# First layer of the first expert put between the count groups of the second routing round

## The chip, the cores and the metric

The kernel runs on one core of a Trainium2 chip. The core has a matrix engine (TensorE, here PE), a vector engine (VectorE, DVE), a scalar engine (ScalarE, ACT), GpSimd (POOL) and a queue engine (SyncE, SP), which work from queues of their own and wait for each other by semaphores. The metric is the device time of one execution, in microseconds (us); lower is better.

## The reference

The reference is attention with sink tokens, then a mixture of experts with greedy routing, then one with Sinkhorn weights. The attention has batch 2, 8 heads, 768 positions, head size 64, a window of 128 and 4 sinks. Its output is seen as 1536 tokens of 512 numbers. The part that the change touches is the greedy routing and its experts:

```python
cap = N // E                                   # 1536 // 8 = 192
flat = (x @ w_gate).flatten()
for idx in np.argsort(-flat):
    tok, e = idx // E, idx % E
    if assigned[tok] >= 0 or counts[e] >= cap: continue
    assigned[tok] = e; counts[e] += 1
for e in range(E):
    mask = assigned == e
    out[mask] = np.maximum(x[mask] @ w1[e], 0.0) @ w2[e]     # w1: 512x1024, w2: 1024x512
```

After it, eight experts are applied to all tokens and summed with weights from eight Sinkhorn steps.

## The kernel before

Attention comes first and fills about the first 150 us. It leaves the gate's logits `L` and, for the first routing round, a count that is made along the way (`first_count`). Then `routing_and_moe1` finds the greedy assignment in eight rounds, each of which closes one expert. In a round every token that is still free proposes to its best open expert. `count` finds for each token how many better proposals its expert has. `route` picks the expert that is filled, and the places of its tokens. `place_tokens` turns the places into a list of token numbers by one-hots (`ohs`) and a product, loads that expert's weights (`load_w`) and gathers its tokens (`gather`). `leave` takes the tokens and the expert out of the preferences `val`. `propose` takes the next maxima and spreads them over the partitions: the products L541 and the copies L542 give `row`.

`count` works on n chunks of 128 tokens, 12 in the first four rounds and 6 after `compact`. For each chunk DVE makes the comparison blocks `gt` (L559) and `g` (L560 and L562), which have four buffers each (`GB`), and PE multiplies them by the proposals into `cnt` (L568). Two chunks (`GC`) make one group of products. Within a group the products are given in reverse, so that they all stand behind the last block that DVE makes.

The expert's layers are in `moe1(r)`: L720 multiplies the gathered and turned tokens `xe` by the first weights in eight blocks of 128 (four matmuls each), ScalarE applies the Relu (L722) into `hT`, L731 multiplies by the second weights, and the gate logits of the next mixture follow (L742). `moe1(r - 1)` is written behind round r, so that its products fill PE during the routing. The weights of an expert come in four parts of 1 MB. Those of the first expert are split: part (0,0), the first half of the first layer, goes by SyncE's queue as soon as the expert is known, and the other three go by ScalarE's queue behind the last copy of `row`. `turn_tokens` (L704, L706) turns the gathered tokens; for the first expert it stands ahead of the second round's count.

The order of the instructions on each engine is set when the kernel is built: a planner takes what is ready by its own estimates, with the routing rounds under `tc.high_priority` ahead of the rest. `tc.issue_after(x)` puts instructions behind `x` on its engine, as an edge of order and not as a wait.

Of the kernel before, what the change touches and what calls it, by code (L numbers as in the profile page):

```python
# [8 lines left out]
F32 = mybir.dt.float32  # L9
# [3 lines left out]
AF = mybir.ActivationFunctionType  # L13
OP = mybir.AluOpType
# [6 lines left out]
def kernel(  # L21
# [16 lines left out]
    nc = tc.nc  # L38
    B, H, S, D = q.shape
    N, DM = out.shape  # L40
    E = moe_w_gate.shape[1]
    F = moe_w1.shape[2]
    P = 128
# [3 lines left out]
    CAP = N // E  # L47
# [15 lines left out]
    KD = DM // P  # L63
    KF = F // P
# [19 lines left out]
    slots = rp.tile([P, HC], BF, name="slots")  # L84
# [32 lines left out]
    val = rp.tile([P, NCH, E], F32, name="val")  # L117
# [300 lines left out]
    pm = ctx.enter_context(tc.tile_pool(name="pm", bufs=1, space=PSUM))  # L418
# [49 lines left out]
    def routing_and_moe1():  # L468
# [3 lines left out]
        mp = cx.enter_context(tc.tile_pool(name="mp", bufs=2))  # L472
# [12 lines left out]
        st = dict(n=NCH, L=L, val=val, code=code, prop=prop0, m=m0)  # L485
# [59 lines left out]
        def count(n, m, prop, row):  # L545

            cnt = ps.tile([P, n, E], F32, name="cnt", bufs=1)

            turned = st.pop("turned", None)
            with nullcontext() if turned is None else tc.issue_after(turned):  # L550
                nc.tensor.matmul(cnt.rearrange("p c e -> p (c e)"), zb, zb[:, :n * E], start=True, stop=False,
                                 skip_group_check=True)
            for c0 in range(0, n, GC):
                c1 = min(n, c0 + GC)
                blocks = []
                for c in range(c0, c1):
                    g = gp.tile([P, n, P], BF, name="g", bufs=GB)
                    gt = gp.tile([P, P], BF, name="gt", bufs=GB)
                    nc.vector.scalar_tensor_tensor(gt, row[:, c], m[:, c:c + 1], before, op0=OP.is_equal, op1=OP.mult)  # L559
                    nc.vector.tensor_scalar(g[:, :c + 1], row[:, :c + 1], m[:, c:c + 1], None, op0=OP.is_lt)  # L560
                    if c + 1 < n:
                        nc.vector.tensor_scalar(g[:, c + 1:], row[:, c + 1:], m[:, c:c + 1], None, op0=OP.is_le)  # L562
                    blocks += [(c, gt, prop[:, c, :])] + [(cc, g[:, cc, :], prop[:, c, :]) for cc in range(n)]

                first = None
                for cc, a, b in reversed(blocks):
                    with nullcontext() if first is None else tc.issue_after(first.ins):
                        mm = nc.tensor.matmul(cnt[:, cc, :], a, b, start=False, stop=(a is blocks[0][1] and c1 == n),  # L568
                                              skip_group_check=True)
                    first = first or mm  # L570
            return cnt
# [34 lines left out]
        def place_tokens(r, ft, t1, eh, code, n):  # L606

            def expert():
                return nc.vector.tensor_scalar(EIX[:, r:r + 1], t1[:, 1:2], -1.0, float(E), op0=OP.mult, op1=OP.add)

            if r == 0:
                expert()
                load_w(0, ((0, 0),))
            nc.vector.tensor_scalar(ft[:, 1], ft[:, 0], HC + 0.5, None, op0=OP.is_gt)
            nc.vector.scalar_tensor_tensor(ft[:, 2], ft[:, 1], -float(HC), ft[:, 0], op0=OP.mult, op1=OP.add)
            sm = ps.tile([P, 512], F32, name="sm", bufs=1)
            ohs = gp.tile([P, n, HC], BF, name="oh", bufs=OB)
            for c in range(n):
                nc.vector.tensor_scalar(ohs[:, c], slots, ft[:, 2, c:c + 1], None, op0=OP.is_equal)
            ch = gp.tile([P, n, 2, 2], BF, name="ch", bufs=OB)  # L620
            nc.vector.tensor_mul(ch[:, :, 1], code, ft[:, 1].unsqueeze(2).to_broadcast([P, n, 2]))
            nc.vector.tensor_sub(ch[:, :, 0], code, ch[:, :, 1])
            first = None
            for c in reversed(range(n)):
                with nullcontext() if first is None else tc.issue_after(first.ins):
                    mm = nc.tensor.matmul(sm[:HC, 0:4], ohs[:, c], ch[:, c].rearrange("p h a -> p (h a)"),
                                          start=(c == n - 1), stop=(c == 0), skip_group_check=True)
                first = first or mm
            st["placed"] = mm.ins
            at = rp.tile([HC, 2], F32, name="at", bufs=2)  # L630
            nc.vector.tensor_reduce(at, sm[:HC, 0:4].rearrange("p (h a) -> p h a", h=2), axis=AX.X, op=OP.add)
            known = nc.vector.tensor_copy(ixs[:, r, :], at)
            gather(r)
            if r:

                with tc.issue_after(known.ins):
                    expert()
                load_w(r, PARTS)

        def leave(ft, eh, n):  # L640

            val = st["val"]
            nc.vector.tensor_scalar(ft[:, 3], ft[:, 0], 0.5, None, op0=OP.is_gt)
            nc.vector.scalar_tensor_tensor(val, eh.unsqueeze(1).to_broadcast([P, n, E]), -100.0, val, op0=OP.mult,
                                           op1=OP.add)
            nc.vector.scalar_tensor_tensor(val, ft[:, 3].unsqueeze(2).to_broadcast([P, n, E]), -1000.0, val,
                                           op0=OP.mult, op1=OP.add)

        W, XG, YT = {}, {}, {}
        JH = KF // 2  # L650
        PARTS = ((0, 0), (0, 1), (1, 0), (1, 1))
        GC, GB = 2, 4
# [37 lines left out]
                nc.scalar.activation(xh, x, AF.Copy)  # L690
                nc.vector.tensor_sub(xl, x, xh.bitcast(F32))

        XE = {}

        def turn_tokens(r):

# [10 lines left out]
            if r == 0:  # L707
                st["turned"] = turned.ins

        def moe1(r):  # L710


            w1, w2 = W.pop(r)
            xe = XE.pop(r)
            hT = mp.tile([P, KF, CAP], F32, name="hT", bufs=1)
            for j0 in range(0, KF, 2):
                ph = pm.tile([P, 2, CAP], F32, name="mm", tag="mm", bufs=3)
                for j in (j0, j0 + 1):
                    for k in range(KD):
                        nc.tensor.matmul(ph[:, j - j0, :], w1[j // JH][:, k, j % JH * P:(j % JH + 1) * P], xe[:, k, :],  # L720
                                         start=(k == 0), stop=(k == KD - 1))
                nc.scalar.activation(hT[:, j0:j0 + 2, :], ph, AF.Relu)  # L722
            if r % 2 == 0:
                YT[r // 2] = mp.tile([P, KD, 2 * CAP], F32, name="yT", bufs=2)
            yT = YT[r // 2]
            s0 = r % 2 * CAP
            for k0 in range(0, KD, 2):
                py = pm.tile([P, 2, CAP], F32, name="mm", tag="mm", bufs=3)
                for k in (k0, k0 + 1):
                    for j in range(KF):  # L730
                        nc.tensor.matmul(py[:, k - k0, :], w2[j // JH][:, j % JH, k * P:(k + 1) * P], hT[:, j, :],  # L731
                                         start=(j == 0), stop=(j == KF - 1))
                nc.scalar.activation(yT[:, k0:k0 + 2, s0:s0 + CAP], py, AF.Copy)
                if k0 == 0 and r + 1 < E:
                    turn_tokens(r + 1)
            operands(r)

            c0, c1 = s0 // P, (s0 + CAP) // P
            pl = ps.tile([P, 2, E], F32, name="lg", bufs=1)
            for a in range(c0, c1):  # L740
                for k in range(KD):
                    nc.tensor.matmul(pl[:, a - c0, :], yT[:, k, a * P:(a + 1) * P], wg2[:, k, :],  # L742
                                     start=(k == 0), stop=(k == KD - 1))
            c = r // 2 * (2 * CAP // P)
            nc.vector.tensor_copy(L2[:, c + c0:c + c1, :], pl[:, :c1 - c0, :])

        for r in range(E):
            with tc.high_priority(offset=HP):
                got = route(r)
                place_tokens(r, *got)  # L750
                leave(got[0], got[2], got[4])
                if r + 1 == E // 2:
                    compact(NC2)
                if r + 1 < E:
                    propose()
                if r == 0:

                    with tc.issue_after(st["shown"]):
                        load_w(0, PARTS[1:], nc.scalar)
                    turn_tokens(0)  # L760
            if r == E - 1:
                rcx.close()
                pools.append(ctx.enter_context(tc.tile_pool(name="stg", bufs=1, side="right", reuse_waits="tile")))
            if r > 0:
                moe1(r - 1)
# [186 lines left out]
```

## Time and profile before

| what | value |
|---|---|
| median of 3 runs | 1417.15 us (1414.22 to 1417.31) |
| profiled execution, its own time | 1415.5 us |
| its span, first to last instruction | 1413.8 us |
| PE busy | 1375.5 us (97%) |
| DVE busy | 835.5 us (59%) |
| ACT busy | 459.8 us (33%) |
| POOL busy | 411.8 us (29%) |
| mean granted clock of PE | 0.984 |

The profile is of one execution; times in it count from its first instruction. A busy share is an average over attention, routing with the first experts (about 150 to 390 us) and the second mixture, which have different limits. Records of matmuls overlap, so their lengths don't add up to time. The granted clock is given as a share of 2.4 GHz.

### The profile page before, as it was taken

What the parts mean: (1) busy time and instruction counts of PE and PEld (TensorE: products, weight loads), DVE (VectorE), ACT (ScalarE), POOL (GpSimd) and SP (SyncE); (2) the same over time, 40 slices, a digit from 0 to 9 for tenths busy, and PEclk for the clock granted to TensorE, in tenths of its full rate; (3) what the DMA queues carried; (4) which work ended last, traced back from release to release, by engine and by line L of the source; (5) the groups of instructions that cost most, each with busy time, mean ns of one, the idle gap of its engine ahead of it and who ended that gap; (6) DMA issues with size and microseconds to landing.
All of it is one profiled execution on the core that took longest, in us unless ns stands there. A gap on an engine that the chain in (4) does not pass through costs nothing.

```text
span 1413.8 us, 20799 instructions
## 1 busy us (share of the span) xinstructions
PE 1375.5 (97%) x8243; PEld 1221.7 (86%) x8243; DVE 835.5 (59%) x1898; ACT 459.8 (33%) x975; POOL 411.8 (29%) x388
## 2 busy tenths in 40 slices
PE   7999599999989999999999999999999999999998
PEld 4667499999978989898889889898988988888987
DVE  4666788860376655555555555555555556555554
ACT  4666112222333332333233323323332332233321
POOL 1136200101332343232223322322343233223303
PEclk9999699999999999999999999999999999999999
DMA  6331343657210010001001100110010001000002
GB/s 141 90 79 39 129 148 131 232 180 227 90 31 31 30 45 31 30 31 45 30 31 32 44 31 30 35 41 30 31 44 32 31 30 45 31 30 31 15 1 89
DMA packets 87225, 87.37 MB, mean 62 GB/s; under 512 B 43864, under 2 KB 60248, under 8 KB 87128
## 3 DMA queue, kind: packets, MB, share of 16 engines
q1 hardware_dynamic: 82056, 73.45, 16.5%
q0 software_dynamic: 2944, 9.44, 2.0%
q10 hardware_dynamic: 2128, 3.16, 0.6%
q8 instruction: 64, 1.05, 0.3%
q14 instruction: 33, 0.27, 0.1%
HBM read 79.75 MB, written 6.30 MB: 61 GB/s over the span
## 4 chain that ended last, share of the span: by engine, by line
PE 93%; DVE 4%; ACT 1%; issue 1%; POOL 0%; DMA 0%; SPq 0%; POOLq 0%; DVEq 0%; ACTq 0%
PE pa L875 37%; PE X L818 19%; PE Z L818 9%; PE mm L720 6%; PE mm L731 6%; PE Y L818 5%; PE S L238 2%; PE o L293 2%; PE PT L280 1%; PE cnt L568 1%; PE ms L305 1%; PE tr L214 1%; PE lg L742 1%; POOL out_dram L888 0%; ACT pb L251 0%
## 5 line engine op out<-in xcount | busy, mean ns | idle before, releaser
L875 PE MATMUL pa<-w,h 128*128 128x512 f32 x2304 | 596.1, 394 | 0.0
L875 PEld LDWEIGHTS pa<-w,h 128*128 128x128 f32 x2304 | 426.9, 188 | 67.5 <-ACT h L825 0.3
L886 DVE SCALAR_TENSOR_TENSOR accs<-pa,Pm,accs 128x512 f32<-128x512 f32 x360 | 269.2, 748 | 212.2 <-PE pa L875 212.2
L826 DVE SCALAR_TENSOR_TENSOR h<-sum,h 128x384 fp32r<-128x384 f32 x192 | 155.4, 809 | 99.6 <-ACT h L825 99.3
L444 POOL TENSOR_TENSOR w1l<-r,w1h 128x512 fp32r<-128x512 f32 x64 | 64.2, 1023 | 450.6 <-ACT w1h L443 415.3
L825 ACT ACTIVATE h<-sum 128x384 fp32r<-128x384 f32 x192 | 100.5, 523 | 207.2 <-DVE sum L835 207.1
L461 POOL TENSOR_TENSOR w<-r,w 128x1024 fp32r<-128x1024 f32 x32 | 77.5, 2422 | 232.4 <-ACT w L460 232.4
L830 ACT ACTIVATE u<-X 128x384 f32<-128x384 f32 x64 | 31.5, 492 | 268.4 <-PE X L818 268.4
L720 PE MATMUL mm<-xe,wf 128*128 128x192 f32 x512 | 95.9, 337 | 0.0
L731 PE MATMUL mm<-hT,wf 128*128 128x192 f32 x512 | 91.5, 331 | 0.0
L444 POOL TENSOR_TENSOR w1l<-S,w1h 128x1024 fp32r<-128x1024 f32 x32 | 86.6, 2705 | 0.0
L720 PEld LDWEIGHTS mm<-xe,wf 128*128 128x128 f32 x512 | 83.1, 192 | 0.1
L731 PEld LDWEIGHTS mm<-hT,wf 128*128 128x128 f32 x512 | 82.6, 190 | 0.5
L835 DVE TENSOR_TENSOR sum<-Z,u 128x384 f32<-128x384 f32 x64 | 35.7, 557 | 58.4 <-ACT u L830 58.4
L668 POOL DMA_INDIRECT xg<-X,ixs x16 | 16.7, 1041 | 168.3 <-PE mm L704 60.6
L830 ACT ACTIVATE v<-X 128x384 f32<-128x384 f32 x64 | 31.4, 491 | 78.7 <-PE X L818 78.7
L251 ACT ACTIVATE pb<-pb,nb 128x264 f32<-128x264 f32 (+1 forms) x96 | 46.5, 489 | 14.2 <-DVE nb L246 14.2
L826 DVE SCALAR_TENSOR_TENSOR h<-X,h 128x384 fp32r<-128x384 f32 x64 | 35.7, 558 | 21.1 <-ACT h L825 21.1
L835 DVE TENSOR_TENSOR sum<-Z,v 128x384 f32<-128x384 f32 x64 | 35.7, 557 | 18.6 <-PE Z L818 18.5
L443 ACT ACTIVATE w1h<-r 128x512 fp32r<-128x512 f32 x64 | 30.2, 519 | 49.3 <-PE Z L818 46.2
L825 ACT ACTIVATE h<-X 128x384 fp32r<-128x384 f32 x64 | 31.5, 492 | 45.0 <-PE X L818 44.9
L241 DVE CUSTOM_DVE_ANT_0 pb<-S,M 128x264 f32<-128x264 f32 (+1 forms) x96 | 36.4, 403 | 13.5 <-PE S L238 12.8
(283 smaller groups left out, 2340.3 us busy)
## 6 DMA issues: line engine op xcount, KB each, us to landing
r<-in_moe_w_dram SPq DMA_DIRECT2D x64, 512.0 KB, 3.4
wf<-in_moe_w_dram SPq DMA_DIRECT2D x29, 1024.0 KB, 6.3
kn<-in_k_dram SPq DMA_DIRECT2D x12, 256.0 KB, 3.5
qn<-in_q_dram SPq DMA_DIRECT2D x12, 256.0 KB, 3.9
vn<-in_v_dram SPq DMA_DIRECT2D x12, 256.0 KB, 3.2
X<-xs POOLq DMA_DIRECT2D x12, 256.0 KB, 2.4
wf<-in_moe_w_dram ACTq DMA_DIRECT2D x3, 1024.0 KB, 10.3
xg<-X,ixs POOLq DMA_INDIRECT x16, 6.1
```

The costliest lines, as they stand in the source:

```text
L251: nc.scalar.activation(PB[c][:, h, :w], PB[c][:, h, :w], AF.Exp, bias=NB[c][:, 0, h:h + 1], scale=scale, accum_out=NB[c][:, 2, h:h + 1])
L444: nc.gpsimd.tensor_sub(w1[1][:, o:o + n], x, w1[0][:, o:o + n].bitcast(F32))
L461: nc.gpsimd.tensor_sub(w2[:, 1], r2, w2[:, 0].bitcast(F32))
L720: nc.tensor.matmul(ph[:, j - j0, :], w1[j // JH][:, k, j % JH * P:(j % JH + 1) * P], xe[:, k, :], start=(k == 0), stop=(k == KD - 1))
L731: nc.tensor.matmul(py[:, k - k0, :], w2[j // JH][:, j % JH, k * P:(k + 1) * P], hT[:, j, :], start=(j == 0), stop=(j == KF - 1))
L818: nc.tensor.matmul(acc_, w1[a][:, o, k, :], XO[x][t][b][:, k, :], start=(start and n == 0), stop=(stop and n == 3 * KH - 1), skip_group_ch ...
L825: nc.scalar.activation(t[:, 0], x, AF.Relu)
L826: nc.vector.scalar_tensor_tensor(t[:, 1], x, 0.0, t[:, 0].bitcast(F32), op0=OP.max, op1=OP.subtract)
L830: nc.scalar.activation(t, x, AF.Copy)
L835: nc.vector.tensor_add(t, a, b)
L875: nc.tensor.matmul(pa, HT[u, f, h][:, a, j * P:(j + 1) * P], w2[:, b, f, :], start=(n == 0), stop=(n == 3 * FP - 1))
L886: nc.vector.scalar_tensor_tensor(acc[:, c], pa, pe, acc[:, c], op0=OP.mult, op1=OP.add)
```

## The change

Of the first expert's first layer, the first four blocks (`EARLY`), sixteen matmuls, are given out at the end of round 0, right behind `turn_tokens(0)` and under the same high priority, and `moe1(0)` makes the rest. In the count of the second round the first product of each group is put behind one of them: the group of chunks 2 and 3 behind the fourth, that of 4 and 5 behind the eighth, that of 6 and 7 behind the twelfth, that of 8 and 9 behind the sixteenth. In all rounds the two operations for `ch` are written ahead of the one-hots, and the first two operations of `leave` are ordered behind the last one-hot; the third needs their results.

```diff
@@ count @@
             turned = st.pop("turned", None)
+            ahead = early if turned is not None else None
...
                 first = None
                 for cc, a, b in reversed(blocks):
-                    with nullcontext() if first is None else tc.issue_after(first.ins):
+
+                    after = first.ins if first else ahead[4 * c0 // GC - 1] if ahead and 0 < c0 <= 4 * GC else None
+                    with nullcontext() if after is None else tc.issue_after(after):
@@ place_tokens @@
-            for c in range(n):
-                nc.vector.tensor_scalar(ohs[:, c], slots, ft[:, 2, c:c + 1], None, op0=OP.is_equal)
             ch = gp.tile([P, n, 2, 2], BF, name="ch", bufs=OB)
             nc.vector.tensor_mul(ch[:, :, 1], code, ft[:, 1].unsqueeze(2).to_broadcast([P, n, 2]))
             nc.vector.tensor_sub(ch[:, :, 0], code, ch[:, :, 1])
+            for c in range(n):
+                shown = nc.vector.tensor_scalar(ohs[:, c], slots, ft[:, 2, c:c + 1], None, op0=OP.is_equal)
+            st["slots"] = shown.ins
@@ leave @@
-            nc.vector.tensor_scalar(ft[:, 3], ft[:, 0], 0.5, None, op0=OP.is_gt)
-            nc.vector.scalar_tensor_tensor(val, eh.unsqueeze(1).to_broadcast([P, n, E]), -100.0, val, op0=OP.mult,
-                                           op1=OP.add)
+            with tc.issue_after(st["slots"]):
+                nc.vector.tensor_scalar(ft[:, 3], ft[:, 0], 0.5, None, op0=OP.is_gt)
+                nc.vector.scalar_tensor_tensor(val, eh.unsqueeze(1).to_broadcast([P, n, E]), -100.0, val, op0=OP.mult,
+                                               op1=OP.add)
@@ moe1 @@
-        XE = {}
+        XE, HT = {}, {}
...
+        EARLY = 4
+
+        def first_layer(r, blocks):
+            w1, xe, hT = W[r][0], XE[r], HT[r]
+            made = []
+            for j0 in blocks:
                 ph = pm.tile([P, 2, CAP], F32, name="mm", tag="mm", bufs=3)
                 for j in (j0, j0 + 1):
                     for k in range(KD):
+                        made.append(nc.tensor.matmul(ph[:, j - j0, :], w1[j // JH][:, k, j % JH * P:(j % JH + 1) * P], xe[:, k, :],
+                                         start=(k == 0), stop=(k == KD - 1)).ins)
                 nc.scalar.activation(hT[:, j0:j0 + 2, :], ph, AF.Relu)
+            return made
...
+            if r not in HT:
+                HT[r] = mp.tile([P, KF, CAP], F32, name="hT", bufs=1)
+                first_layer(r, range(0, KF, 2))
+            else:
+                first_layer(r, range(EARLY, KF, 2))
+            w2 = W.pop(r)[1]
+            del XE[r]
+            hT = HT.pop(r)
@@ round 0 @@
                     turn_tokens(0)
+                    HT[0] = mp.tile([P, KF, CAP], F32, name="hT", bufs=1)
+                    early = first_layer(0, range(0, EARLY, 2))
```

## Rows read from the trace of the kernel before

**Rows 1.** The page, part 4: the chain that ended last, by engine.

```profile
PE 93%; DVE 4%; ACT 1%; issue 1%; POOL 0%; DMA 0%; SPq 0%; POOLq 0%; DVEq 0%; ACTq 0%
```

**Rows 2.** Busy time by stretches: length, engines (instructions), granted clock, DMA share, GB/s.

```profile
150.00:177.00 27.00, 12.39 (x163) 10.01 (x164) 21.72 (x81) 2.94 (x6) 6.54 (x10) 0.50 0.46 163
172.00:176.40 4.40, 0.89 (x27) 0.80 (x28) 4.40 (x11) 0.00 (x0) 0.00 (x0) 0.50 1.04 397
240.00:391.00 151.00, 150.92 (x1191) 147.43 (x1190) 72.94 (x280) 38.38 (x80) 26.29 (x23) 1.00 0.52 171
```

**Rows 3.** PE's waits in 150 to 184 us: total, times, longest.

```profile
PE sm L626 <- DVE ch L622: 4.6, 1, 4.6
PE cnt L568 <- DVE g L562: 3.9, 3, 1.8
...
PE bc L541 <- DVE m L534: 0.7, 1, 0.7
```

**Rows 4.** PE in order of time: start, us, line; in brackets the wait.

```profile
171.09 0.48 PE L568 MATMUL cnt<-prop,g 128*128 128x8 bf16 x12 [0.28 <-DVE g L562]
...
173.73 0.48 PE L568 MATMUL cnt<-prop,g 128*128 128x8 bf16 x12 [1.78 <-DVE g L562]
...
176.37 0.48 PE L568 MATMUL cnt<-prop,g 128*128 128x8 bf16 x12 [1.78 <-DVE g L562]
```

**Rows 5.** The chain that ended last, in order of time: start, us, what.

```profile
177.23 2.77 PE mm L720 x8
...
180.64 2.06 PE mm L720 x12
182.69 0.63 PE cnt L568 x26
```

**Rows 6.** Busy time by stretches, around the rise of the clock.

```profile
179.50:180.00 0.50, 0.50 (x9) 0.33 (x8) 0.50 (x2) 0.00 (x0) 0.00 (x0) 0.50 0.00 0
180.00:180.50 0.50, 0.50 (x26) 0.50 (x23) 0.50 (x4) 0.00 (x0) 0.00 (x0) 0.91 0.00 0
```

**Rows 7.** First weight part: issue by time, us to landing; ScalarE around `xe`.

```profile
160.46 0.40 SPq L661 DMA_DIRECT2D wf<-in_moe_w_dram  x1
...
wf<-in_moe_w_dram SPq DMA_DIRECT2D x1, 1024.0 KB, 4.9
...
169.96 0.87 ACT L706 ACTIVATE xe<-mm 128x384 f32<-128x384 f32 x2 [2.54 <-PE mm L704]
```

**Rows 8.** DVE in order of time: placing of round 0, count, end of count.

```profile
158.49 0.25 DVE L644 SCALAR_TENSOR_TENSOR val<-eh,val 128x96 f32<-128x96 f32 x1
...
158.94 0.17 DVE L614 TENSOR_SCALAR ft<-ft 128x12 f32<-128x12 f32 x1
159.02 0.17 DVE L643 TENSOR_SCALAR ft<-ft 128x12 f32<-128x12 f32 x1
...
159.74 0.25 DVE L646 SCALAR_TENSOR_TENSOR val<-ft,val 128x96 f32<-128x96 f32 x1
159.91 1.94 DVE L619 TENSOR_SCALAR oh<-slots,ft 128x96 bf16<-128x96 bf16 x12
161.76 0.16 DVE L622 TENSOR_TENSOR ch<-code,ch 128x24 bf16<-128x24 bf16 x1
...
163.07 0.16 DVE L631 TENSOR_REDUCE at<-sm 96x2 f32<-96x4 f32 x1 [0.69 <-PE sm L626]
...
173.59 0.35 DVE L559 SCALAR_TENSOR_TENSOR gt<-row,m,before 128x128 bf16<-128x128 f32 x1
...
178.61 0.35 DVE L562 TENSOR_SCALAR g<-row,m 128x256 bf16<-128x256 f32 x1
...
180.45 1.01 DVE L560 TENSOR_SCALAR g<-row,m 128x1536 bf16<-128x1536 f32 x1
183.36 0.26 DVE L583 SCALAR_TENSOR_TENSOR sel<-cnt,prop 128x96 f32<-128x96 f32 x1 [1.90 <-PE cnt L568]
```

**Rows 9.** Waits in 183 to 400 us, DVE's for the counts: total, times, longest.

```profile
DVE sel L583 <- PE cnt L568: 6.4, 5, 1.9
```

More of the change, by code (lines that the diff above doesn't have):

```diff
@@ L708, in turn_tokens @@
                 st["turned"] = turned.ins
[L710 to L716, printed above, removed]
+        EARLY = 4
[3 more added lines that the diff above has]
+            for j0 in blocks:
                 ph = pm.tile([P, 2, CAP], F32, name="mm", tag="mm", bufs=3)
@@ L719, in moe1 @@
                     for k in range(KD):
-                        nc.tensor.matmul(ph[:, j - j0, :], w1[j // JH][:, k, j % JH * P:(j % JH + 1) * P], xe[:, k, :],
-                                         start=(k == 0), stop=(k == KD - 1))
+                        made.append(nc.tensor.matmul(ph[:, j - j0, :], w1[j // JH][:, k, j % JH * P:(j % JH + 1) * P], xe[:, k, :],
+                                         start=(k == 0), stop=(k == KD - 1)).ins)
                 nc.scalar.activation(hT[:, j0:j0 + 2, :], ph, AF.Relu)
+            return made
+        def moe1(r):
+            if r not in HT:
[6 more added lines that the diff above has]
+            hT = HT.pop(r)
             if r % 2 == 0:
```

## The prediction

> **What bounds the kernel now.** I read the page first, then a table by stretches, the waits, and the order of time around the touched code. The chain that ended last lies to 93% on TensorE (PE) [rows 1], so the time is PE's work plus whatever PE waits for. The table [rows 2] says where it waits: from 240 to 391 us it is busy 150.92 of 151.00, but in 150 to 177 us only 12.39 of 27, at a granted clock of 0.50, the lower of its two levels (1.2 GHz). That stretch is the first round of routing and most of the second round's count, and it is the only part of the first MoE where work handed to PE can shorten the run.
>
> What PE waits for there is listed in [rows 3]: 4.6 us for the one-hots, 3.9 us in three pieces for `g`. In order of time [rows 4] the second round's count comes in groups of 26 matmuls (two chunks, 12+1 each); call them G0 to G5. G1 has a wait of 0.28 us, G2 and G3 each have one of 1.78, because VectorE (DVE) needs 2.64 us for two chunks of `g` (173.73 to 176.37). Only behind G3 does the first expert's layer (L720) begin, at 177.23 us in the chain by time [rows 5]. From there PE has no wait: eight L720, G4, twelve, G5, eight more.
>
> Two lengths must be kept apart. The records of L720 overlap, so what counts is how many fit into a stretch: 12 into 2.06 us at full clock, 0.172 each, and 8 into 2.77 us at the lower one, 0.346 each [rows 5]. A count group takes 0.63 us at full clock [rows 5] and 0.86 at the lower one (176.37 [rows 4] to 177.23). The clock rose near 180.05 us: 0.50 until 180.0, 0.91 in the half microsecond after it [rows 6], PE having run without a gap since 176.37.
>
> **The change, part by part.** *Sixteen L720 matmuls given out ahead.* They are the first four 128-wide blocks of the hidden layer, four matmuls each; none is added, so what counts is when they run. Of their operands, the weight part (0,0) is issued by SyncE at 160.46 us and lands 4.9 us later, at 165.4, and `xe` is copied by ScalarE from 169.96 us in 0.87 us, behind its own three weight issues [rows 7]. So they can run from about 170.4 (first half of `xe`) and 170.8 us. The other three parts, 3.15 MB at 397 GB/s [rows 2], take 7.9 us from 169.9, so until about 178 us nothing but these sixteen can be given to PE. No DMA is added or moved past another queue. The two Relu copies fall on a ScalarE that stands idle.
>
> The new edges hold G1 behind the fourth, G2 behind the eighth, G3 behind the twelfth, G4 behind the sixteenth. I take the order to be G0, four, G1, four, G2 and so on, and walk it at the lower clock with everything 0.15 us earlier (next part). G0 ends at 170.65. Four (4 x 0.346 = 1.38) and a group (0.86) take 2.24 us: G1 ends at 172.9, G2 at 175.1, G3 at 177.4, the last four at 178.75. DVE offers two chunks every 2.64 us, those for G2 at 173.6 and for G3 at 176.2, when PE is still at the four ahead of them (to 174.3 and 176.5), so PE doesn't idle. Queued behind each four is a group, and who waits for the group is DVE, by its four `g` buffers: chunk 6 can be written once G1 is done, 172.9, and DVE comes to it at 173.44 (173.59 before [rows 8]); so DVE isn't held, with 0.5 us to spare. G4's `g` is ready at 178.81 (178.61 + 0.35 - 0.15 [rows 8]), G4 ends at 179.65; G5's is ready at 181.31 (180.45 + 1.01 - 0.15), and G5 ends at 182.0. Before, G5 stood behind twelve L720 and ended at 183.32 (182.69 + 0.63 [rows 5]), and DVE idled 1.90 us for it [rows 8]. **First term: 1.32 us**, the 0.15 included.
>
> Second, the L720 done by then: 20 before; now 16 and those that fit between 179.65 and 181.31, 9 at full clock or 4 at the lower one. After nine us without a gap I take the full clock there, and 8 of them, hence 24. **Second term: 4 x 0.172 = 0.69 us.** Bounds: at the lower clock with 8 squeezed in, G5 slips to 183.3 and only the four are gained, 0.7 us in all; with twelve at full clock G5 slips by 0.4 and eight are gained, 2.3. Above all this stands what PE lost there at all: 3.84 us of waits, 4 x 0.23 for G0 to G3 and 8 x 0.174 for eight L720 at the lower clock, 6.1 us.
>
> The FP8 and Floating Point Precision page of the Trainium skill (TensorE Precision Notes) says that a true FP32 product takes four passes; 192 columns in four passes are, as an estimate from that page, 0.32 us at full clock and 0.64 at the lower one. By that four would take 2.56 us, and with a group 3.42, longer than DVE's 2.64: G5 would end near 186, some 2.7 us late, a rule against the change. The spacing of 0.172 in this trace doesn't bear it out.
>
> *`ch` ahead of the one-hots, `leave` behind them.* Ahead of the twelve one-hots DVE now runs L644, L643 and L646 (0.25, 0.17, 0.25 us), and behind them L622, for which PE's L626 waits [rows 8]. By the starts, L646 holds the one-hots up by 0.17 (159.74 to 159.91). L644 and L643 run where DVE would mostly have waited for the result before (L614 starts 0.45 behind L644, with a reduction between); I take 0.07 for both. L622 costs 0.07 behind the one-hots (it ends at 161.92, they at 161.85) and 0.18 ahead of them, since it needs L621's result. Net 0.17 + 0.07 + 0.07 - 0.18 = 0.13; I take **0.15 us**, once, in the first round. Bounds: 0, and the three whole, 0.67. Behind the one-hots the three cost some 0.45 us ahead of the next proposal, but there DVE idled 0.69 us until PE's L626 was done [rows 8], which hides them; with that cover gone, `m` and the row broadcast L541 would come 0.3 us later (0.45 - 0.15). In later rounds PE is full and the 0.15 is worth nothing.
>
> VectorE: DVE Perf Modes of the Trainium skill (The DRAIN you can't avoid) holds that the next operation doesn't start until the pipe is empty; then each of the three would free its whole length, this part would be worth 0.67 and the sum 2.5. That L643 starts 0.08 behind L614 in this trace [rows 8] speaks against it.
>
> **Sum:** 1.32 + 0.69 = 2.0 us. After G5 PE is the bound until 391 us, and DVE has room: in the later rounds it waits 6.4 us in five pieces for the counts alone [rows 9]. So the lead is kept. The profiled execution took 1415.5 us (span 1413.8), which becomes 1413.5; the median of the runs shown is 1.65 us higher, so against it I forecast 1417.15 - 2.0 = **1415.1 us**.
>
> **The rivals.** *A: the sixteen run as one block behind G0.* No edge holds them behind a group, and all are ready together. Then they end at 170.65 + 16 x 0.346 = 176.2, G1 at 177.0; DVE stops ahead of chunk 6 from 173.44 to 177.0, and G5 ends near 185.6, 2.3 us later than before. But PE has no gap: from 177.9 (G2) to 185.6, less 3 x 0.63, it does 33 more L720, 49 in all, against 30 before at that time. That is 19 x 0.172 = 3.3, less 0.45 for the two steps of routing (`sm`) that it is behind, 2.8 us won, as long as DVE's room [rows 9] takes up the 2.3. Time 1414.3. For it: readiness; against it: nothing in the trace of before.
>
> *B: the moved `leave` shows on PE.* If no L720 stands between L626 and L541 in the new order, PE meets an `m` that is 0.3 us later, up to 0.67 if the three count whole, in each of seven proposals: 2.1 to 4.7 us lost against 2.0 won, 1417.3 to 1419.9, slower; it decides from 0.29 us a round on. For it: PE waited 0.7 us for `m` in the first round [rows 3]. Against it: later no PE wait is in the table [rows 2].
>
> *C: the gain is only a swap.* The order behind G4 loses the L720 that went ahead, PE idles until G5, and 16 stand against 20: 1.32 - 0.69 = 0.6 us, time 1416.5. For it: PE's queue holds only what the order gives it, as the 1.78 us waits show [rows 4].
>
> *D: PE's lead is larger*, with the full clock from G1 on and L720 in every gap: up to 6.1 us, 1411.1.
>
> **How the numbers follow.** Main case 0.45, A 0.18, B 0.12, C 0.17, D 0.08. The likeliest gives 1415.1, its own range 1414.3 to 1416.5. The runs shown spread over 3.1 us, so 0.3% (4.25 us) is about what can be told from no change. 1411.6 to 1418.6 leaves out the end of D, the upper part of B and some scatter. Faster by over 0.3% needs D, or A with scatter: 0.14. Slower by over 0.3% needs more than B's upper end, an order I don't foresee: 0.07. Within 0.3%: 0.79.
>
> **What would show it.** Right: L720 from about 170.6 us on, the 1.78 us waits for `g` gone, G5 ending near 182, DVE's 1.90 us wait at L583 cut to about 0.7, the span near 1411.8, PE still full to 391. A full clock before 178 would speak for D; a DVE gap near 173.5 with a block of sixteen for A; a wait of L541 for `m` in later rounds for B; a PE wait ahead of G5 for C. The forecast is wrong if the new order moves other work of the first MoE too, which the trace of before can't show.

## Result and the profile after

The changed kernel takes 1429.55 us (median of 4 runs, 1429.15 to 1434.15) against 1417.23 us before; the ratio is 1.0103, interval 1.0089 to 1.0117. It is slower by 1%, 12.3 us by the medians and 14.6 by the ratio, which is not that of the medians, where 2 us were to be won; that is outside the range. The profiled execution is the longest of the four, 1434.15 us with a span of 1432.4.

To see where the time went I cut each trace at two starts that every version has: the copy of the first count (L361, on DVE) and the first product of the Sinkhorn part (`gmx` on PE). Columns are us; "route 1 to 3" are the starts of the product `sm<-red` of the second to fourth round, counted from that copy.

| kernel | up to the copy | copy to Sinkhorn | behind it | route 1 | route 2 | route 3 |
|---|---|---|---|---|---|---|
| before | 154.7 | 247.2 | 1011.9 | 29.9 | 57.5 | 84.2 |
| after | 156.5 | 262.1 | 1013.8 | 32.1 | 68.3 | 105.1 |

Of 18.6 us, 14.9 lie in the first MoE; the attention, which the change doesn't touch, took 1.8 more in this execution, and the part behind 1.9. The second routing is 2.2 us late, the third 10.7, the fourth 20.9. PE's waits from 150 to 400 us say what stands there now (line, what it waited for: total, times, longest):

```profile
PE mm L709 <- DMA xg<-X,ixs: 9.1, 5, 4.4
...
PE bc L541 <- DVE m L534: 1.3, 1, 1.3
```

The 3.9 us of waits for `g` [rows 3] are gone, as forecast. In their place stand 9.1 us for `xg`, the gathered tokens, 8.3 of them behind the first round, where no wait was before. Here is PE in order of time:

```profile
172.73 2.93 PE L724 MATMUL mm<-xe,wf 128*128 128x192 f32 x8 [0.26 <-ACT xe L711]
175.46 0.51 PE L571 MATMUL cnt<-prop,g 128*128 128x8 bf16 x12
...
176.20 2.72 PE L724 MATMUL mm<-xe,wf 128*128 128x192 f32 x8
178.75 0.44 PE L571 MATMUL cnt<-prop,g 128*128 128x8 bf16 x12
...
197.10 1.14 PE L748 MATMUL mm<-hT,wf 128*128 128x192 f32 x6
202.67 0.42 PE L709 MATMUL mm<-ident,xg 96*128 96x96 f32 x1 [4.43 <-DMA xg<-X,ixs]
203.42 1.38 PE L709 MATMUL mm<-ident,xg 96*128 96x96 f32 x7 [0.33 <-DMA xg<-X,ixs]
204.59 2.18 PE L748 MATMUL mm<-hT,wf 128*128 128x192 f32 x6
206.57 0.51 PE L571 MATMUL cnt<-prop,g 128*128 128x8 bf16 x12
```

Two things are to be seen. The products ahead stand where I put them, eight records, a group, eight records, a group. And at 198.2 us PE comes to the turning of the second expert's tokens (L709) and stands for 4.8 us. Behind it in the queue wait 32 records of the second layer (L748) and the third round's first count group, whose last block DVE has made by 200.6 us. The chunks' buffers are not freed, so DVE stops too. By stretches (granted clock is the third number from the end):

```profile
198.20:202.70 4.50, 0.07 (x2) 0.03 (x1) 3.77 (x7) 0.49 (x1) 0.00 (x0) 0.98 1.05 358
202.70:207.00 4.30, 3.97 (x29) 3.56 (x30) 0.00 (x0) 1.39 (x3) 0.00 (x0) 0.50 1.05 403
```

After that stand PE works at the lower clock, 0.50. DVE, busy 3.77 of the 4.5 us, is then held up for the whole of 202.7 to 207. The next round repeats it (2.6 and 1.0 us). From 185 to 300 us the mean granted clock is 0.93 where before it was 1.00: some 16 us at half speed, an estimate from these two means of up to 8 us lost beside the 8.3 us of waits; the lead that PE had won pays a part of it back.

Why the gather is late is in GpSimd's rows and in the DMA share of the stretch, 1.05:

```profile
195.12 0.92 POOL L673 DMA_INDIRECT xg<-X,ixs  x1 [26.89 <-DVE pl L533]
196.34 0.92 POOL L673 DMA_INDIRECT xg<-X,ixs  x1 [0.30 <-PE bc L541]
...
xg<-X,ixs POOLq DMA_INDIRECT x2, 7.3
```

It takes 7.3 us to land (median of the two), while 4 MB of the same expert's weights are on the DMA engines; in the first round of before, where hardly any weights ran beside it (their first part landed at 165.4, a microsecond behind the issue of the gather), it took 3.1. In the second round of before, beside the same 4 MB, it was slow too, 6.3 us, but PE came late enough:

```profile
192.51 0.92 POOL L668 DMA_INDIRECT xg<-X,ixs  x1 [0.30 <-issue]
...
195.45 0.44 PE L568 MATMUL cnt<-prop,g 128*128 128x8 bf16 x12
...
197.49 0.45 PE L568 MATMUL cnt<-prop,g 128*128 128x8 bf16 x12
...
199.85 0.66 PE L704 MATMUL mm<-ident,xg 96*128 96x96 f32 x6
```

Before, PE came to this place 45.1 us behind the copy of the first count, with the second gather issued at 37.8; now at 41.7, with the gather issued at 39.8. PE is 3.4 us earlier, the gather 2.0 later, and the margin, about a microsecond before, has become a wait of 4.8. Of the 3.4 some 1.3 come from the order: two count groups of the third round stood ahead of the turning before (195.45 and 197.49) and stand behind it now.

### The profile page after: what moved, and what is told of

The parts are those of the page before. It is cut to its first block, busy times and chain, and to the rows that moved or that the text cites. A ratio compares the mean times of both kernels' runs of the same rounds, so it can differ in the third digit from the quotient of the medians.

```text
span 1432.4 us, 20802 instructions
## 1 busy us (share of the span) xinstructions
PE 1390.5 (97%) x8243; PEld 1232.7 (86%) x8243; DVE 838.4 (59%) x1898; ACT 460.8 (32%) x975; POOL 410.5 (29%) x388
## 3 DMA queue, kind: packets, MB, share of 16 engines
q8 instruction: 64, 1.05, 0.3%
## 4 chain that ended last, share of the span: by engine, by line
PE 92%; DVE 4%; DMA 2%; issue 1%; ACT 1%; POOL 1%; SPq 0%; ACTq 0%; POOLq 0%; DVEq 0%
PE pa L894 37%; PE X L837 18%; PE Z L837 9%; PE mm L724 6%; PE mm L748 6%; PE Y L837 5%; PE S L238 2%; PE o L293 2%; PE PT L280 2%; DMA xg<-X,ixs 1%; PE cnt L571 1%; PE ms L305 1%; PE tr L214 1%; PE lg L759 1%; POOL out_dram L907 0%
## 5 line engine op out<-in xcount | busy, mean ns | idle before, releaser
L748 PE MATMUL mm<-hT,wf 128*128 128x192 f32 x512 | 98.3, 342 | 0.0
L748 PEld LDWEIGHTS mm<-hT,wf 128*128 128x128 f32 x512 | 86.2, 198 | 0.3
L854 DVE TENSOR_TENSOR sum<-Z,v 128x384 f32<-128x384 f32 x64 | 35.7, 557 | 18.6 <-PE Z L837 18.5
```

What stands on the lines that cost most here:

```text
L854: nc.vector.tensor_add(t, a, b)
```

## The experiments

**The two parts alone.** First the order of `ch` and `leave`, without the products ahead:

```diff
+            for c in range(n):
+                shown = nc.vector.tensor_scalar(ohs[:, c], ...)   # behind ch
+            st["slots"] = shown.ins
...
+            with tc.issue_after(st["slots"]):                     # leave, first two operations
```

> The kernel before with the order of place_tokens and leave changed alone. Theory 1 (TensorE comes too soon to the turning of the next expert's tokens and its queue stands until their gather lands; this needs the products given ahead): within 0.3% of before, 1414 to 1420 us, no wait of TensorE for a gather of over 1 us behind the first round. Theory 2 (leave behind the one-hots delays m and the rows in every round): most of the loss is here, 1423 us or more.

Measured: 1421.94 us, ratio 1.0045 (1.0028 to 1.0061). Neither theory: TensorE has no long wait for a gather, as theory 1 says (0.6 us once, in the first round), but the part is no neutral one. DVE's rows (of the whole change, this part is the same there) show why:

```profile
164.72 0.16 DVE L635 TENSOR_REDUCE at<-sm 96x2 f32<-96x4 f32 x1 [0.68 <-PE sm L630]
164.80 0.24 DVE L531 TENSOR_REDUCE mx<-val 128x12 f32<-128x96 f32 x1
...
165.66 0.25 DVE L534 TENSOR_REDUCE m<-pl 128x12 f32<-128x96 f32 x1
```

In the kernel before they stood so:

```profile
161.85 0.24 DVE L531 TENSOR_REDUCE mx<-val 128x12 f32<-128x96 f32 x1
162.12 0.26 DVE L532 SCALAR_TENSOR_TENSOR prop<-val,mx 128x96 bf16<-128x96 f32 x1
...
163.43 0.25 DVE L534 TENSOR_REDUCE m<-pl 128x12 f32<-128x96 f32 x1
```

There `mx` and `prop` ran ahead of `at` and so during its wait of 0.69 us [rows 8]. With `leave` behind the one-hots the planner puts `at` first; it waits for PE, and `mx` to `m` stand behind it. The wait that was to hide the three operations now stands ahead of what they delay. Counted from the copy of the first count, `m` starts at 9.15 us instead of 8.71, 0.44 later, where I forecast 0.15 earlier. Route 1 is at 32.0 (before 29.9), Sinkhorn at 250.8 (247.2).

`ch` alone, ahead of the one-hots, with `leave` as it was:

> The kernel before with ch ahead of the one-hots alone, leave as before. If the loss of the run with both was in leave, moved behind the one-hots and so behind the reduction that waits for TensorE: within 0.3% of before, 1413 to 1418 us, m at the same time behind the first count to 0.2 us. If it was in ch: 1419 us or more.

Measured: 1417.84 us against 1416.06, ratio 1.0019 (1.0008 to 1.0030), inside the expectation; PE's order is that of before, from the copy to the end, and Sinkhorn is at 248.1. So most of this part's loss comes with `leave`.

Then the products ahead with their edges, `ch` and `leave` in the old order:

> The kernel before with the sixteen products ahead and their edges alone, leave and ch in the old order. Theory 1: as slow as the whole change, 1426 to 1434 us, with the waits of 4 to 5 us and 2 to 4 us for the gather in the second and third round. Theory 2: within 0.3% of before.

Measured: 1428.34 us, ratio 1.0087 (1.0067 to 1.0107), as theory 1 says. PE's waits of this kernel:

```profile
PE mm L707 <- DMA xg<-X,ixs: 10.6, 6, 3.5
```

**The turning later in PE's queue.**

```diff
-                if k0 == 0 and r + 1 < E:
+                if k0 == KD - 2 and r + 1 < E:
                     turn_tokens(r + 1)
```

> The whole change, but the turning of the next expert's tokens is written behind the second half of the second layer instead of the first, so that sixteen more products and some count groups stand ahead of it. Theory 1: the waits for the gather go, and with them 8 us and the lower clock behind them: 1414 to 1421 us. Theory 3 (the count groups held behind the sixteen make the routing late, and that is the loss): stays at 1425 us or more, since the groups are held as before.

Measured: 1418.09 us, ratio 1.0014 (1.0004 to 1.0024): 1.03% has become 0.14%. The same stretch of this kernel, by busy time, which in the changed kernel has PE at 17.21 of 22 us and a clock of 0.84:

```profile
190.00:212.00 22.00, 21.97 (x260) 20.92 (x259) 19.76 (x57) 5.06 (x10) 1.84 (x2) 1.00 0.57 210
```

PE has no wait there any more; the copy to Sinkhorn takes 247.3 us, as before. Theory 3 falls: route 1 is as late as in the whole change (32.0), and the time is back all the same. The control, the late turning alone in the kernel before:

> The kernel before with the late turning alone, the control for the late turning. TensorE had no wait at the turning before, so nothing is to be won: 1414 to 1418 us. If the late turning is a gain of its own, 1412 us or less, and then it is no proof for theory 1.

Measured: 1416.2 us against 1416.06, ratio 1.0011 (0.9996 to 1.0025). It gains nothing by itself. And with the products ahead, but `leave` in the old order:

> The products ahead and their edges, leave and ch in the old order, the turning of the next tokens behind the second half of the second layer. Theory 1 (the loss is TensorE's queue standing at the turning) with leave as a smaller loss of its own: 2 to 4 us below the whole change with the late turning, 1412 to 1416 us, no wait for the gather over 1 us behind the first round. If the count groups held behind the products cost what the late routing suggests (2 us): 1416 to 1419 us.

Measured: 1416.02 us, ratio 0.9994 (0.9985 to 1.0003): 2.1 us below the median of the run with the new order of `leave`, and the same as before.

**The gather faster.** The turning stays where it is; SyncE's queue reads a few bytes of the gathered tiles ahead of the weights, and so waits for them:

```diff
+                for x in XG[r]:
+                    nc.sync.dma_start(seen[r:r + 1, :], x[0:1, 0:4])
                 load_w(r, PARTS)
```

> The whole change, and in each round but the first SyncE's queue reads a few bytes of the two gathered tiles ahead of the next expert's weights, so that these 4 MB start when the gather has landed. TensorE's order hardly changes. Theory 1 with the weights as what makes the gather slow: it lands about 3 us after its issue instead of 7, the two waits fall to about 1 us each and the clock stays up: 1417 to 1423 us. If the gather is as slow without the weights beside it: 1428 us or more.

Measured: 1427.48 us, ratio 1.0073 (1.0050 to 1.0097). This is no answer, because the edit didn't do what it was meant to. SyncE's queue in this kernel:

```profile
197.92 0.38 SPq L669 DMA_DIRECT2D wf<-in_moe_w_dram  x1
204.78 0.31 SPq L644 DMA_DIRECT2D seen<-xg  x1
205.28 0.40 SPq L669 DMA_DIRECT2D wf<-in_moe_w_dram  x1
```

One part of 1 MB had gone ahead of the reads, and beside it the gather took 6.6 us. With the weights ordered behind the second read:

```diff
+                for x in XG[r]:
+                    landed = nc.sync.dma_start(seen[r:r + 1, :], x[0:1, 0:4])
+                with tc.issue_after(landed.ins):
+                    load_w(r, PARTS)
```

> As the run that held SyncE's queue until the gather had landed, but now all four parts of the weights are ordered behind that; in the run before one part of 1 MB had slipped ahead. If the weights are what makes the gather slow, it lands some 3 us after its issue, the waits at the turning fall to 1 to 2 us and the time to 1420 to 1425 us. If the gather takes 5 us by itself, 1426 us or more.

Measured: 1415.9 us against 1416.06, ratio 1.0003 (0.9993 to 1.0014): the whole loss is gone, more than I expected. PE's order is that of the changed kernel, from the copy to the end; its rows, and SyncE's and the gather's:

```profile
196.88 1.14 PE L752 MATMUL mm<-hT,wf 128*128 128x192 f32 x6
199.17 0.30 PE L713 MATMUL mm<-ident,xg 96*128 96x96 f32 x1 [1.15 <-DMA xg<-X,ixs]
199.63 0.80 PE L713 MATMUL mm<-ident,xg 96*128 96x96 f32 x7 [0.16 <-DMA xg<-X,ixs]
...
199.14 1.35 SPq L644 DMA_DIRECT2D seen<-xg  x2
201.54 2.28 SPq L670 DMA_DIRECT2D wf<-in_moe_w_dram  x4
...
xg<-X,ixs POOLq DMA_INDIRECT x2, 3.8
```

The gather lands in 3.8 us instead of 7.3, the stand of 4.8 us is one of 1.3, and the clock stays at 1.00 in this stretch. The routing stays late (the fourth round 6.5 us, table below), so its lateness alone isn't the loss. The Trainium skill (DMA: Bandwidth & Descriptors, Issuing engines are not separate DMA queues) says that transfers started by different engines run on the same 16 DMA engines and interleave. The traces agree: GpSimd's gather takes 7.3 us beside SyncE's weights and 3.8 with these held back.

**What is left to win.** Three combinations and one control, each against a before of 1416.95 us. First the products ahead with their edges and the weights held, `ch` and `leave` in the old order:

> The products ahead with their edges, leave and ch in the old order, all weights of the later rounds ordered behind the gather. Theory 1 (the weights slow the gather that TensorE's queue stands at): the 10.6 us of waits fall to some 3 us, 1412 to 1417 us, so 10 us or more below the same kernel without the hold. Otherwise 1424 us or more.

Measured: 1415.25 us, ratio 0.9990 (0.9980 to 1.0001); waits for the gather 2.7 us instead of 10.6, as expected. The same with the late turning:

> As the run before it in this call, and the turning late as well: no wait for the gather behind the first round at all. If the lead that TensorE wins by the products is kept, 1412 to 1415 us, the fastest so far; if the routing, held up by the same products, eats it, the same as before, 1415 to 1418 us.

Measured: 1416.41 us, ratio 0.9987 (0.9975 to 0.9998). By its ratio the fastest of all, 0.13%, at the edge of what can be told; the median is only 0.5 us below the kernel before's, and inside the range that was given for no gain. The control, the weights held in the kernel before:

> The kernel before with the weights behind the gather alone, the control. TensorE had no wait for the gather behind the first round, so nothing changes: 1413 to 1418 us.

Measured: 1418.37 us, ratio 1.0004 (0.9994 to 1.0013): no gain without the products ahead, 0.4 us above the range expected. And the kernel with products ahead and weights held, without the edges:

```diff
-                    after = first.ins if first else ahead[4 * c0 // GC - 1] if ahead and 0 < c0 <= 4 * GC else None
+                    after = first.ins if first else None
```

> The products ahead without the edges, so that the planner sets them as one block of sixteen behind the fourth count group; old leave, weights behind the gather. If the edges make the second round's count late (by 1 to 2 us), the second routing comes earlier than with them by that much in spite of the block, and the time is 1412 to 1416 us; if the block holds the last groups up as much, no difference to the kernel with the edges.

Measured: 1417.91 us, ratio 1.0002 (0.9993 to 1.0011). The expectation missed: route 1 comes at 32.8, later than the 31.1 with the edges, and Sinkhorn at 248.9 against 246.2. In these traces the block of sixteen behind the fourth group is worse than the spread; by the times, whose intervals touch, that isn't settled.

The cuts of the other kernels, as in the first table:

| kernel | copy to Sinkhorn | behind it | route 1 | route 2 | route 3 |
|---|---|---|---|---|---|
| `ch` and `leave` alone | 250.8 | 1014.5 | 32.0 | 60.4 | 89.3 |
| `ch` alone | 248.1 | 1012.1 | 30.7 | 58.3 | 85.1 |
| products ahead alone | 258.9 | 1012.0 | 31.0 | 66.8 | 101.3 |
| whole change, late turning | 247.3 | 1014.5 | 32.0 | 59.9 | 88.5 |
| whole change, weights held | 247.6 | 1012.1 | 31.9 | 61.9 | 90.7 |
| products, late turning | 246.2 | 1012.2 | 30.4 | 57.7 | 87.2 |
| products, weights held | 246.2 | 1012.2 | 31.1 | 60.2 | 88.3 |
| late turning alone | 247.3 | 1011.3 | 30.6 | 58.3 | 86.3 |
| weights held alone | 248.0 | 1012.6 | 30.7 | 58.3 | 85.0 |

The kernels with `ch` alone and with the weights held alone have PE's order of before throughout, and yet their route 1 is 0.8 us and their Sinkhorn 0.8 to 0.9 us later than in the profiled execution of before. In that one the clock rose 25.4 us behind the copy, in these two at 27.2 and 27.3. So differences of this size between two rows are not the edit's.

## Why the prediction was wrong, step by step

*Where PE waits, and that filling the gaps takes the waits away:* right. The waits for `g` went, and the order was the one I walked, but that the last of the four fours ran between the products of G3.

*The price of the four products: wrong by a factor of two.* "0.172 each" is the price of a record, and a matmul of this type leaves two. The page after shows it as well as the one before:

```profile
L724 PE MATMUL mm<-xe,wf 128*128 128x192 f32 x512 | 96.9, 342 | 0.3 <-ACT xe L711 0.3
```

Eight experts of eight blocks of four matmuls are 256, and 512 records are there. So four cost 2.73 us at the lower clock (172.73 to 175.46), not 1.38, and with a group 3.5 (to 176.20), longer than DVE's 2.64 for two chunks. DVE, which was to have 0.5 us to spare, is held by its buffers, and G5's wait, which was to shrink to 0.7, is nearly as long as before:

```profile
179.26 0.35 DVE L560 SCALAR_TENSOR_TENSOR gt<-row,m,before 128x128 bf16<-128x128 f32 x1 [0.49 <-PE cnt L571]
...
182.94 0.35 DVE L560 SCALAR_TENSOR_TENSOR gt<-row,m,before 128x128 bf16<-128x128 f32 x1 [0.95 <-PE cnt L571]
...
187.34 0.26 DVE L586 SCALAR_TENSOR_TENSOR sel<-cnt,prop 128x96 f32<-128x96 f32 x1 [1.79 <-PE cnt L571]
```

G5 comes 2.2 us later instead of 1.3 earlier. By the parts alone, route 1 is at 31.0 with the products and at 32.0 with `ch` and `leave`, against 30.7 in the two kernels with PE's order of before, so the larger share of the delay is that of `leave`, and the doubled price cost little here: with the products alone the clock rose 20.2 us behind the copy, 7 us sooner than in those two. The rule of the Trainium skill that I set aside (FP8 and Floating Point Precision, TensorE Precision Notes, four passes) came within 8% of the trace: two records of 0.172 make 0.344 us a matmul at full clock, and 2.73/4 = 0.68 at the lower one, against the 0.32 and 0.64 estimated from that page.

*The second term, the L720 done by G5's end: mis-sized.* 48 records stand ahead of G5, 20 before. That is the 24 matmuls of the forecast, but the "20 before" were records, ten matmuls. So PE had won 28 x 0.172 = 4.8 us of work by G5's end, not 0.7; as G5 came 2.2 us later, that is a lead of some 2.6.

*The `leave` part: wrong in sign.* The placing did come earlier as forecast: `at` starts 8.21 us behind the copy instead of 8.35, 0.14 where 0.15 was taken. The cover named for the rest, DVE's 0.69 us, was real too, but the operation that waits moved ahead of those it was to cover. Rival B named the sign and the place, and put it in every round on PE; it showed as a later `m` and a later second round, 3.6 us up to Sinkhorn, or 2.7 to 2.8 against the two kernels with PE's order of before.

*"So the lead is kept" is the step that failed.* I asked whether DVE had room and not what PE would meet next in its queue. PE came to an operation that waits for a transfer 3.4 us sooner, the transfer was issued 2.0 us later, and the queue stood there with work behind it: 8.3 us of waits and the lower clock behind them, 14.9 us lost up to Sinkhorn. That the order of other work could move, as the turning and two count groups did, the prediction's last sentence had left open. That the order in the queue makes the loss is shown twice, by the late turning with its control and by the faster gather; that the weights make the gather slow is shown by the pair of holds. No rival named it: A held PE to be full as long as DVE had room, and D, the lead, counted it as pure gain. How the loss divides between the waits and the clock was not measured apart.

*Size.* With the trap taken away the products ahead bring about 0.1%, at the edge of what can be told: of the three kernels with `leave` in the old order and the edges, only one has an interval without 1 in it (0.9975 to 0.9998). By the cuts it is 1.1 to 1.8 us against the controls (246.2 against 247.3 with the late turning alone and 248.0 with the weights held alone), little more than two executions with one order differ by. That this is about what I forecast for the main case is luck, since both terms and the `leave` part were off. Where the rest of the lead goes is in part open. With the late turning the clock falls to 0.50 from 236.8 to 240.2 us and from 298.2 to 301.6, though PE stands nowhere there, an estimate of up to 3.4 us lost; with the weights held the gather still costs PE 1.3 us more than in the control.

## What to carry to other kernels

Work that fills an engine's idle time also brings that engine sooner to the next thing in its queue. Look for the first instruction there that waits for a transfer, take its margin, and compare it with the lead: here a margin of about 1 us met a shift of 5.4, of which 3.4 were the engine's and 2.0 the transfer's. Before using a spacing as a price, divide the records in the profile by the instructions in the code.

## What the hardware showed that I had not expected

A gather of 2 x 96 rows lands in 3.1 us when the weights are held behind it (products ahead, second round), in 6.3 (before) and 7.3 (after) beside 4 MB of weights issued at the same time, and in 6.6 beside 1 MB.

The part behind Sinkhorn, in which the versions have the same work, took 1011.3 to 1012.6 us in most profiled executions and 1013.8 to 1014.5 in three. In the two shown below PE stands at its start for 3.7 us and some 30 us on for 2.7, and works at the lower clock behind that; how long differs. From 390 to 450 us, the kernel before and then `ch` and `leave` alone:

```profile
390.00:450.00 60.00, 53.40 (x261) 46.53 (x261) 41.78 (x99) 23.68 (x46) 21.11 (x16) 0.94 0.12 32
```

```profile
390.00:450.00 60.00, 53.41 (x254) 47.15 (x253) 38.37 (x95) 21.83 (x43) 18.91 (x15) 0.89 0.10 27
```

A mean of 0.94 against 0.89 with the same busy time is some 6 us more at half speed, and the latter execution's part behind Sinkhorn is 2.6 us longer. Which of the two an execution gets was not taken apart, so 2.6 of the 6.7 us by which the profiled execution of `ch` and `leave` alone is longer can't be put down to the edit.
